# Chunk attention and a token mixer on one core: units of 512 tokens and four heads in place of 256 tokens and eight, q and k in 1 KB pieces, and transposes of 64x64

## The chip, the cores and the metric

The kernel runs on one core of a Trainium2 chip. The metric is the device time in microseconds of that core, the median of the runs. The engines are named as the profile names them: PE (matmul; PEld is its weight load), DVE and ACT (vector and scalar work; both can read PSUM), POOL (here it issues the loads, which cast float32 to float16 on the way) and SP (here it issues the stores). PSUM has 8 banks of 512 float32 per partition, called `ps` in the code.

## The reference, cut to what matters

```python
# q, k, v: (8 batches, 8 heads, 576 tokens, 64); each chunk of 64 tokens attends to itself
scores = scale * np.matmul(q_c, k_c.transpose(0, 1, 2, 4, 3))     # 9 chunks of 64x64 a head
scores = scores - np.max(scores, axis=-1, keepdims=True)
attn = np.exp(scores)
attn = attn / (np.sum(attn, axis=-1, keepdims=True) + 1e-09)
out = np.matmul(attn, v_c)
...
x = out.transpose(0, 2, 1, 3).reshape(B, S, H * D)                # (8, 576, 512)
wq = x @ w_q                                                      # (8, 576, 64)
wk = x @ w_k
W_tok = scale * np.einsum('bsd,btd->bst', wq, wk)
mixed = np.einsum('bst,btd->bsd', W_tok, x)
return (np.maximum(mixed, 0.0) @ w_out).astype(np.float32)
```

## The kernel before, in words

The mixer is linear up to its relu, so for each batch the kernel first makes the 64x512 matrix G = wk^T x over all 576 tokens, and then relu(wq G) w_out for each stretch of tokens.

**Units.** A unit is a pair of 128-token tiles of one batch, with all eight heads: two for each batch (512 tokens), and four "rest" units, each with the last 64 tokens of two batches. That makes 20 units (`pairs`, line 148). A unit is worked in these steps; each step is one entry of a graph and is emitted as a whole:

- `tq` (line 365, `tqr` at 349 for a rest): q, and likewise k, lies with two tokens in one partition (`R = 2`). PE transposes 128x64 pieces by the identity, 16 for each of q and k; two go side by side into the two halves of PSUM's partitions.
- `qb`, `kt` (line 287, the helper `copy`): q goes to SBUF in two copies of 64 partitions, into a block-diagonal tile `qbd` that is zero elsewhere; k in one copy.
- `S` (389): 16 matmuls of 64 columns with the block-diagonal q as 128x128 weights, so that two heads come out of one matmul. Scores fill two banks.
- `mx`, `sub` (402, 412), both DVE: row maximum over the keys, then the subtraction, which also puts the tokens of a chunk back into order (it reads PSUM in order and writes with a step of 2). `exp` (422), ACT.
- `E` (434): 8 transposes of 128x128. `et` (287): copy to SBUF.
- `V` (464), two steps: 16 matmuls of 64x64 weights and 65 columns each, in the four quarters of the array by turns; the 65th column of v is 1 and gives the denominator. `den`, `rec`, `x` (477, 481, 491), all DVE: add 1e-9, reciprocal, multiply into `xs`.
- `xT`, `xt` (511, 287), `pj`, `wt` (521, 287), `wkT`, `wk` (538, 287): x transposed, projected by w_q and w_k at once, and wk turned back.

When all units of a batch are there, `G` (575) and its two copies `gx`; then for each unit `mix` (616), `rm` (629 on DVE, 631 on ACT; relu with the scale), `out` (643, four matmuls of 512 columns for 128 tokens), `osb` (287, the eviction) and the store (226). An `out` step with i = 1, or of a rest unit, is stored as two halves of 64 rows, since its two chunks lie apart or in other order: 40 stores have 64 rows, 16 have 128.

**What sets the order.** `ORDER` (line 20) is written out by hand: each word is a step's number, the engine (P, V or S; `copy` steps may go to either V, DVE, or S, ACT) and the PSUM bank. Words `w7` or `n7` are idle matmuls of 512 or 128 columns that keep PE's clock up. Each engine works through its own instructions in this order and waits on semaphores. `LOADS` (line 60) is the order of the loads; POOL issues them in this order through `graph.queue` (97), each as soon as the words before it have emitted the step that frees its buffer. There are 7 homes for q and k pairs and 10 for v pairs. The first q and k come through SP as float32 and are cast (line 303). `GATE` (66, 280): a small DMA on SP reads the last load's data; all stores stand behind it on SP's queue, so no store starts before the loads are done. Up to 24 output tiles (`osb`) can wait.

Of the kernel before, what the change touches and what calls it, by code (L numbers as in the profile page):

```python
# [9 lines left out]
F16 = mybir.dt.float16  # L10
# [10 lines left out]
5V 4V 0S 1S w7 w7 w7 w7 n7 n7 n7 n7 n7 n7 n7 n7 n7 n7 n7 n7 6P0 2V 3S 7V w7 n7 n7 n7 n7 n7 n7 n7 n7  # L21
9P1 8S n7 n7 34P2 10S 35S 11P0 31P2 12V 32S 13V 33S w7 w7 n7 n7 n7 n7 n7 n7 n7 n7 56P3 36P4 58S 14S
59V 37V n7 n7 n7 91P2 57S 15P0 92S 60P3 38V 94P1 93S 95S 61V 39S w7 n7 n7 n7 n7 n7 96P4 62V 116P1
16S 97V 40P3 63S 21P6 41S 64P0 98V 118S 17P2 65S 18V 22V 99S 66P4 23V 19V 24V 117S 67V 20V 100P0
42P6 68V 46P2 69V 25P1 43V 47V 70P4 44V 26S 45V 101S 48V 71S 49V w5 n5 n5 n5 n5 n5 119P1 102P4 120S
106P2 50P0 107V 108V 27P1 109V 51S 72P6 28S 103V 52P0 73S 74P1 29P6 121P2 53S 75V 54P0 30V 163P1
122V 55S 76P0 164S 160P6 77V 104V 78S 105V 79P0 123V 80S 110P7 85P4 124S 83P0 86V 111S 125P1 84S
81P4 126V 161S 162S 127P0 131P2 112P5 128V 132V 129V 133V 89P6 130V 113S 82S 134V 165P0 90S 114P4
135P2 166V 87P3 136S 137P2 167V 88S 138S 210P5 139P2 295P3 115V 140S 211V 168S 141P0 212V 185P1 213V
142S 298V 214P2 143S 169P4 186S 215V 144P6 170V 188P0 145S 216V 150P4 189S 187V 175P6 146P2 296S  # L30
176V 217S 297V 177V 190P0 178V 147S 380P3 151S 191V 218P2 245P6 219V 247S 299P4 192V 248P5 246S
148P2 249S 300V 193S 152P0 301V 149S 382V 220P6 171P4 153S 194P1 221V 172V 173V 383S 154P2 222V 195S
223V 381S 174V 200P0 155S 196P6 224P3 201V 156P4 202V 197V 225S 203V 179P2 226P3 198V 180S 199V
250P0 302S 181P2 157V 204P6 251V 182S 303P4 205S 158P2 304S 227S 252V 183P5 384P4 184S 206P3 159S
228P5 330P6 207S 229V 208P0 332V 273P1 209S 253S 230P0 385V 358P2 331S 231V 270P3 274V 232S 271S
386V 233P0 359S 272V 305P6 333P4 234S 306V 307V 275P2 308V 334S 239P0 276V 237P5 240S 254P4 277V
238S 335P0 255S 241P5 336V 278S 355P2 242S 256P6 337V 279P3 357S 309P4 280S 243P5 257V 258V 356S
259V 281P0 310S 285P2 244S 260P6 282V 235P4 283V 286V 338S 261V 284V 311P5 262V 287V 360P0 263V 312S
236S 339P5 288V 387S 264P6 361V 289P2 265S 388P3 313P4 290S 266P6 362V 291P2 267S 340S 268P6 415P7
389S 314V 269S 292S 390P0 345P4 293P2 391V 418P3 346V 294S 347V 363S 392V 348V 315P2 443P6 393V 316S  # L40
341P4 419S 394P0 342V 364P1 317S 343V 395V 416S 318P2 344V 396P0 365S 417V 324P4 349P1 325V 350S
444S 397V 366P4 319S 370P0 440P6 367V 368V 371V 509P7 372V 441S 373V 420P2 369V 442S 320P0 421V 511S
351P1 510S 374P4 352V 321S 445P6 422V 375S 326P1 446V 376P0 423S 322P2 327S 377V 424P3 447V 398P0
353P1 378P4 399S 484P5 354S 487P0 379V 323S 425V 400P1 448S 488V 430P2 426P6 485S 328P4 431V 432V
427V 433V 486S 449P0 428V 329V 402S 489P2 401S 429V 403P4 490V 434P1 404S 409P6 450S 491V 556P4 410S
512P5 553P0 557V 435S 455P2 451P6 513S 405P1 456V 457V 492S 452V 458V 514P4 453V 406S 454V 407P2
555S 515V 459P1 554S 493P3 460S 408V 436P0 494S 461P1 516V 437S 495P2 462S 499P6 578P0 496V 500V
517S 497V 581P1 501V 498V 558P4 502V 580S 463P2 518P3 559V 579S 438P6 503P7 582S 411P0 504V 464S
439S 519S 465P1 560V 412S 520P2 466S 524P6 413P0 521V 467S 525V 522V 523V 561S 474P4 526V 583P2 527V
475S 505P1 584V 562P6 506S 468P4 528P1 585V 469S 476P7 414S 480P4 529V 470P2 586S 481V 507P0 530P1  # L50
477V 563S 587P3 508S 531S 564P4 588V 568P0 532P6 482P7 533S 569V 565V 471S 570V 566V 571V 534P3 483S
567V 589P0 536S 593P6 572P2 590V 535S 591V 594V 592V 478P4 573S 595V 596V 549P0 574P2 550V 597P3
575S 543P6 598V 472P0 544S 479V 599P1 547P2 600V 601P1 576P3 537P4 602S 577S 545P6 538S 603P1 548S
551P3 605V 473V 541P2 552S 604V 546S 606P0 542S 612P4 607V 539P3 613S 618P6 608P0 619S 540S 620P1
609V 616P2 621S 610P0 617V 614P1 611S 615S
# [5 lines left out]
k1 q1 rk0b rq0b rk0a rq0a q3 k3 q4 v0a v0b rv0b v1a rv0a v1b k4 v3a v3b wq wk k5 q5 wo v4b v4a rk1b  # L61
rq1b rq1a rk1a q6 k6 v5b v5a q8 k8 rv1a rv1b v6a v6b q11 k9 q9 k12 k11 v8a v14a q16 v9a q12 v9b v8b
v19a k15 k14 v12a q14 v11a v11b v12b v19b q15 v18a q17 q18 v14b k18 k17 v15b v17b k16 v17a q19 v15a
v18b v16a k19 v16b
"""
GATE = 76
# [28 lines left out]

# [18 lines left out]
def kernel(  # L114
# [10 lines left out]
    nc = tc.nc  # L125
# [3 lines left out]
    C, P, R, G = 64, 128, 2, 32  # L129
    NF = DM // P  # L130
    HP = H // 2
    NPB = S // (2 * P)
# [4 lines left out]
    NB2 = B // 2  # L137
# [10 lines left out]
    pairs = []  # L148
    for b in range(B):
        pairs += [(b, m) for m in range(NPB)]  # L150
        if b in (0, 2, 3, 4):
            pairs.append((b, None))
    index = {bm: u for u, bm in enumerate(pairs)}
    rests = [u for u, (b, m) in enumerate(pairs) if m is None]
    whole = [u for u, (b, m) in enumerate(pairs) if m is not None]
    both = [(0, 1)] + [(b, b + 3) for b in (2, 3, 4)]
    rest_of = {b: (rests[n], c) for n, bs in enumerate(both) for c, b in enumerate(bs)}
    NQK, NV = 7, 10

    RINGS = {  # L160
        "qb": 3, "kt4": 3, "kt2": 2, "mx2": 3, "mx1": 2, "sh2": 2, "sh1": 1, "es2": 2, "es1": 1,
        "et2": 2, "et1": 1, "xs2": 8, "xs1": 4, "xt2": 2, "xt1": 1, "wt2": 8, "wt1": 4, "wk": 8,
        "wkr": 4, "rm2": 4, "rm1": 1, "g16": 5, "den": 4, "rec": 4, "osb": 24,
# [10 lines left out]
    qbd = [const.tile([P, HP, 4, 2, C], F16, name=f"qbd{n}") for n in range(RINGS["qb"])]  # L174
    g16 = [const.tile([P, DM], F16, name=f"g16{n}") for n in range(RINGS["g16"])]
    wkr = [const.tile([P, 2, DH], F16, name=f"wkr{n}") for n in range(RINGS["wkr"])]
    qk_homes = [const.tile([P, 2, H, R * D], F16, name=f"qk{n}") for n in range(NQK)]
    wo = const.tile([P, NF, DM], F16, name="wo")
    v_all = const.tile([P, 2 * NV, H, VW], F16, name="v_all")
    v_rest = const.tile([P, NB2, H, VW], F16, name="v_rest")  # L180
    gate = const.tile([1, 1], F16, name="gate")
    qkr = const.tile([P, 2, NB2, H, D], F16, name="qkr")
    ones = const.tile([P, 512], F16, name="ones")
    for t, value in [(ones, 1.0)] + [(t, 0.0) for t in qbd[:2]]:
        nc.vector.memset(t[:], value)
# [8 lines left out]


    qk = {u: qk_homes[n % NQK] for n, u in enumerate(whole)}
    st, wide, turned, valued = {}, {}, {}, {}

    def rows_of(x, u):
        b, m = pairs[u]  # L200
        return x[b, :, 2 * P * m : 2 * P * m + 2 * P, :].rearrange("h (p r) d -> p h (r d)", r=R)

    def load_qk(u, t):
        nc.gpsimd.dma_start(qk[u][:, t], rows_of((q, k)[t], u))  # L204

    def v_home(u, i):
        return v_all[:, 2 * (whole.index(u) % NV) + i]

    def load_v(u, i):
        b, m = pairs[u]  # L210
        of = v[b, :, 2 * P * m + P * i : 2 * P * m + P * i + P, :].rearrange("h p d -> p h d")
        nc.gpsimd.dma_start(v_home(u, i)[:, :, 0:D], of)  # L212

    def load_rest(x, part, c):
        b, n = (c, 1) if part == 0 else (2 + 3 * c, NB2 - 1)
        of = (q, k, v)[x][b : b + n, :, S - C : S, :].rearrange("b h p d -> p (b h) d")
        to = v_rest if x == 2 else qkr[:, x]
        to = to[half(c), part : part + n, :, 0:D].rearrange("p n h d -> p (n h) d")
        nc.gpsimd.dma_start(to, of)

    held = []

    def store(to, of):

        if "open" in st:
            nc.sync.dma_start(to, of)
        else:
            held.append((to, of))

    def open_gate(of):  # L230
        nc.sync.dma_start(gate[:], of)
        st["open"] = True
        for to, x in held:
            nc.sync.dma_start(to, x)

    def load_w(i, x):
        nc.gpsimd.dma_start(wqk[:, :, i, :], x.rearrange("(f p) j -> p f j", p=P))

    for t, x in enumerate((q, k)):
        for i in range(2):  # L240
            wide[t, i] = ring([P, DM], F32, "osb")
            rows = rows_of(x, 0)[:, 4 * i : 4 * i + 4]
            nc.sync.dma_start(wide[t, i][:].rearrange("p (h e) -> p h e", e=R * D), rows)
            graph.loads.append((f"f{t}{i}", "SP", 512))
# [5 lines left out]
    for t in wkr:  # L250
        nc.gpsimd.memset(t[:], 0.0)
# [456 lines left out]
```

## Time and profile before

| | |
|---|---|
| runs | 138.96, 141.2, 141.28 us; median 141.2 |
| span of the profiled execution | 138.2 us; its own time is not listed apart from the span |
| busy | PE 121.3, DVE 107.2, ACT 99.9, POOL 70.3 us |
| DMA | 25.11 MB in 86185 packets, 182 GB/s over the span |
| POOL's queue (loads) | 78544 packets, 14.29 MB as they land |
| SP's queue (first loads, stores) | 7618 packets, 10.49 MB |

How to read it: a row of a group is line, engine, operation, output<-input, shapes, count | busy us, mean ns of one | idle time ahead of it and what ended it. The mean of a PE row contains its way through the array; what one matmul costs in a row of them is read from the chain of work that ended last, whose rows are start, duration and count. A stage row is from:to, length, then busy us and count of PE, PEld, DVE, ACT and POOL, the granted clock, the DMA share and GB/s. Loads count with the bytes that land, half of what is read, because they are cast to float16.

### The profile page before, as it was taken

The numbers are of one execution on the slowest core, as the hardware profiler recorded it, in microseconds if no ns is written. First come the engines' busy times: TensorE is split into PE (matmuls) and PEld (weight loads), VectorE is DVE, ScalarE is ACT, GpSimd is POOL, SyncE is SP. The second block draws the span as 40 slices with busy tenths as digits, with TensorE's granted clock in tenths as the row PEclk, the third lists the DMA queues.
The fourth block names the chain that finished last, engine by engine and source line by source line (L and its number), as shares of the span: only waits on it lengthen the run. The fifth ranks groups of instructions, "written<-read, shape, count | busy, mean of one in ns | idle before, by whom it ended". The sixth has DMA issues, their size and how long they took to land.

```text
span 138.2 us, 5123 instructions
## 1 busy us (share of the span) xinstructions
PE 121.3 (88%) x2184; PEld 88.0 (64%) x2184; DVE 107.2 (78%) x212; ACT 99.9 (72%) x186; POOL 70.3 (51%) x93
## 2 busy tenths in 40 slices
PE   5839996998999999999999949998999999999800
PEld 2627784785578757777677838677785866645300
DVE  6443699879698999999998969999999989644200
ACT  3333699656868988889998939697999886468400
POOL 8999999965658479587959867200000000000000
PEclk9975799999999999999999999999999999999995
DMA  3999999999999999999999999992788596888895
GB/s 113 228 162 178 164 158 162 187 180 137 143 165 175 150 163 183 174 166 168 173 165 167 177 173 170 165 142 22 197 249 254 155 312 196 283 267 181 235 283 143
DMA packets 86185, 25.11 MB, mean 182 GB/s; under 512 B 78994, under 2 KB 81554, under 8 KB 86162
## 3 DMA queue, kind: packets, MB, share of 16 engines
q0 software_dynamic: 78544, 14.29, 140.4%
q1 hardware_dynamic: 7618, 10.49, 26.3%
q8 instruction: 17, 0.28, 0.8%
q14 instruction: 6, 0.05, 0.1%
HBM read 29.62 MB, written 9.44 MB: 283 GB/s over the span
## 4 chain that ended last, share of the span: by engine, by line
PE 67%; ACT 15%; DVE 5%; DMA 5%; issue 3%; SPq 1%; ACTq 0%
PE ps L643 20%; PE ps L365 9%; PE ps L521 6%; PE ps L389 5%; PE ps L616 5%; PE ps L511 5%; PE ps L434 5%; DMA osb<-in_k_dram 5%; PE ps L464 5%; ACT es L422 4%; PE ps L575 3%; ACT qbd L287 3%; ACT et L287 2%; DVE sh L412 2%; PE ps L675 2%
## 5 line engine op out<-in xcount | busy, mean ns | idle before, releaser
L643 PE MATMUL ps<-wo,rm 128*128 128x512 f16 x144 | 36.2, 379 | 0.3 <-ACT rm L631 0.2
L212 POOL DMA_DIRECT2D v_all<-in_v_dram x32 | 28.4, 894 | 7.9 <-DMA v_all<-in_v_dram 2.0
L402 DVE TENSOR_REDUCE mx<-ps 128x16 f32<-128x1024 f32 (+1 forms) x20 | 22.2, 1111 | 4.6 <-PE ps L389 4.1
L491 DVE TENSOR_TENSOR xs<-ps,rec 128x512 f16<-128x512 f32 x36 | 24.1, 686 | 0.5
L365 PE MATMUL ps<-ident,qk 128*64 128x128 f16 x512 | 21.3, 230 | 3.2 <-DVE qk L287 1.6
L365 PEld LDWEIGHTS <-qk 128*64 128x64 f16 x512 | 16.8, 115 | 6.3 <-ACT qk L287 1.8
L422 ACT ACTIVATE es<-sh 128x1024 f16<-128x1024 f32 (+1 forms) x20 | 19.5, 977 | 1.4 <-DVE sh L412 1.1
L643 PEld LDWEIGHTS <-rm 128*128 128x128 f16 x144 | 12.5, 98 | 11.6 <-ACT rm L631 0.8
L412 DVE TENSOR_TENSOR sh<-ps,mx 128x1024 f32<-128x1024 f32 x16 | 19.6, 1222 | 0.3
L287 ACT COPY osb<-ps 128x512 f32<-128x512 f32 x29 | 16.7, 587 | 3.5 <-PE ps L643 3.3
L287 ACT COPY qbd<-ps 64x512 f32<-64x512 f32 (+1 forms) x31 | 16.9, 551 | 3.3 <-PE ps L365 1.9
L631 ACT ACTIVATE rm<-ps 128x1024 f16<-128x1024 f32 (+1 forms) x14 | 13.9, 996 | 3.4 <-PE ps L616 3.2
L204 POOL DMA_DIRECT2D qk<-in_k_dram x15 | 13.5, 902 | 4.4 <-DMA wo<-in_moe_w_out_dram 1.8
L204 POOL DMA_DIRECT2D qk<-in_q_dram x15 | 13.4, 896 | 2.8 <-DMA qk<-in_q_dram 0.9
L287 ACT COPY xt<-ps 128x512 f32<-128x512 f32 (+1 forms) x16 | 8.7, 547 | 5.4 <-PE ps L511 5.1
L616 PE MATMUL ps<-wt,g 128*128 128x256 f16 (+1 forms) x96 | 11.2, 246 | 1.6 <-issue 1.0
L389 PE MATMUL ps<-kt,qbd 128*128 128x64 f16 x288 | 12.1, 196 | 0.1
L389 PEld LDWEIGHTS <-qbd 128*128 128x128 f16 x288 | 10.6, 100 | 1.7 <-issue 0.5
L464 PEld LDWEIGHTS <-et 64*64 64x64 f16 x576 | 7.5, 107 | 6.1 <-issue 2.3
L511 PE MATMUL ps<-ident,xs 128*128 128x128 f16 x144 | 11.1, 219 | 0.0
L521 PE MATMUL ps<-xt,wqk 128*128 128x256 f16 (+1 forms) x80 | 10.8, 261 | 0.0
L434 PE MATMUL ps<-order,es 128*128 128x128 f16 x128 | 9.8, 219 | 1.0 <-ACT es L422 1.0
(59 smaller groups left out, 176.6 us busy)
## 6 DMA issues: line engine op xcount, KB each, us to landing
out_dram<-osb SPq DMA_DIRECT2D x40, 128.0 KB, 2.6
v_all<-in_v_dram POOLq DMA_DIRECT2D x32, 128.0 KB, 8.5
out_dram<-osb SPq DMA_DIRECT2D x16, 256.0 KB, 2.6
qk<-in_k_dram POOLq DMA_DIRECT2D x15, 256.0 KB, 8.9
qk<-in_q_dram POOLq DMA_DIRECT2D x15, 256.0 KB, 8.9
osb<-in_q_dram SPq DMA_DIRECT2D x2, 256.0 KB, 3.1
osb<-in_k_dram SPq DMA_DIRECT2D x2, 256.0 KB, 5.9
wo<-in_moe_w_out_dram POOLq DMA_DIRECT2D x1, 512.0 KB, 8.7
```

The lines of the kernel that those rows point to most:

```text
L204: nc.gpsimd.dma_start(qk[u][:, t], rows_of((q, k)[t], u))
L212: nc.gpsimd.dma_start(v_home(u, i)[:, :, 0:D], of)
L287: (nc.vector.tensor_copy if eng == DVE else nc.scalar.copy)(to, of)
L365: nc.tensor.transpose(tp[half(o), j, :, r, :], of, ident[:])
L389: nc.tensor.matmul(sp[:, i, j, c, :], lhsT=st["qb", u][:, j, x].rearrange("p o s -> p (o s)"), rhs=st["kt", u][:, j, x * C : x * C + C], s ...
L402: nc.vector.tensor_reduce(mx[:], scores(), axis=AX.X, op=ALU.max)
L412: nc.vector.tensor_tensor(out=sh[:].rearrange("p x (g r) -> p x r g", r=R), in0=in_banks(bs, 512).rearrange("p i (x r g) -> p (i x) r g", ...
L422: nc.scalar.activation(es[:].rearrange("p x s -> p (x s)"), st["sh", u][:].rearrange("p x s -> p (x s)"), AF.Exp, scale=scale_attn,)
L491: nc.vector.tensor_tensor(out=to, in0=xp()[:, :, :, 0:D], in1=by, op=ALU.mult)
L521: nc.tensor.matmul(pj, lhsT=wqk[:, f].rearrange("p i j -> p (i j)"), rhs=st["xt", u][:, f, :], start=(f == 0), stop=(f == NF - 1),)
L616: nc.tensor.matmul(ma[:, o, f, s], lhsT=st["g", bb][:, (2 * o + f) * P : (2 * o + f) * P + P], rhs=st["wt", u][:, s], start=True, stop=True,)
L643: nc.tensor.matmul(in_banks(bo, DM)[:, 0], lhsT=rm[:, f, i * P : i * P + P], rhs=wo[:, f, :], start=(f == 0), stop=(f == NF - 1),)
```

## The change

It rewrites the units, and with them nearly every function; `Step`, `Banks`, `Graph` and the launch stay.

- **Units.** A unit is 512 tokens of one batch and four heads (`HQ`), two for each batch; a rest unit is the last 64 tokens of four batches, all heads (batches 8 and 9 in the code). That makes 18 units of 32 chunk-heads each. The order of the batches is 0, rest 8, 1, 2, 3, rest 9, 4 to 7 (`TOKENS`).
- **q and k** lie with four tokens in one partition (`R = 4`): a piece is 1 KB of DRAM, and one load brings q or k of a whole batch. Batch 0 comes half through SP (as float32), half through POOL. There are 4 homes. v has a place for every batch (no reuse).
- **Transposes** (`QUART_T` names all units): 64 of 64x64 a unit, in the quarters of the array, q and k together into two banks; **one copy** of 128x1024 takes them to SBUF (`qkT`). There is no block-diagonal tile. `S` is 32 matmuls of 64x64 weights and 64 columns in quarters.
- **The subtraction** reads PSUM with the four tokens' order undone: `p (r g)` as `p g r`, so neighbours in its output are 16 words apart in PSUM, in runs of four; it writes without a step.
- `pj`, `wt`, `wkT`, `wk`, `mix` and `rm` are worked for a batch (512 columns) rather than for a unit.
- **Loads held in line** (`look`, `INLINE`): before a load is issued, POOL copies one element of the load ahead of which, by the table `rates`, 7 us of loading lie; so POOL waits there until that load has landed.
- **Stores.** All whole units' outputs are stored as 128 rows; only the four rest outputs go in halves. After the last load, stores go by turns to POOL's and SP's queue. The gate stands at load 60 of 63 (the second piece of v of batch 7).
- **A new order**: 505 steps in place of 622, 60 idle matmuls of 512 columns, 26 of them before the first transpose and none after the first words of batch 2.

```diff
-GATE = 76
+GATE = 60
+YS = ((0,), (1,))
+OUTS = (1, 1, 1, 1)
+MIX = 2
+QUART_T = [(b, w) for b in range(10) for w in range(2)]
+INLINE = 7.0
...
-    C, P, R, G = 64, 128, 2, 32
+    C, P, R = 64, 128, 4
+    HQ = H // 2
+    G = C // R
+    NT = 4
...
+    TOKENS = [0, 8, 1, 2, 3, 9, 4, 5, 6, 7]
+    NQK = 4
...
+    def load_qk(t, b, part):
+        nc.gpsimd.dma_start(qk[b][:, t, hs(part)], rows_of((q, k)[t], b)[:, hs(part)])
...
+    def send(to, of):
+        if st.get("last") and count["pool"] < count["sp"]:
+            count["pool"] += 1
+            nc.gpsimd.dma_start(to, of)
+        else:
+            count["sp"] += 1
+            nc.sync.dma_start(to, of)
...
+    def look(of):
+        nc.gpsimd.tensor_copy(peek[0:1, :], of)
...
+        rates = {256: 14.5, 512: 22.9, 1024: 39.7, 2048: 73.0}
+        line.append((n * rates[size] / 16000, last))
+        seen = next((m for m in range(n_load, -1, -1) if sum(x for x, _ in line[m:]) > INLINE), -1)
+        if 0 <= seen < n_load and INLINE:
+            graph.queue.append((lambda of=line[seen][1]: look(of()), lambda: []))
...
-                for j in range(HP):
-                    for r in range(R):
-                        for o in range(2):
-                            of = qk[u][:, t, 2 * j + o, r * D : r * D + D]
-                            nc.tensor.transpose(tp[half(o), j, :, r, :], of, ident[:])
...
+            def pe_t(eng):
+                tp = in_banks(bt, 512, F16).rearrange("p a (t j y r g) -> p a t j y r g", t=2, j=2, y=4, r=R)
+                for t in (1, 0):
+                    for j in range(2):
+                        for n in range(4):
+                            for a, o in QUARTERS:
+                                if rest < 0:
+                                    of = qk[b][half(a), t, HQ * w + 2 * j + o, n * D : n * D + D]
+                                    to = tp[half(o), a, t, j, :, n, :]
...
+                                nc.tensor.transpose(to, of, ident[half(a), half(a)])
...
+        def ev_t(eng):
+            tt = ring([P, 2, 2, 2, 4, C], F16, "qkT")
+            to = tt[:].rearrange("p b j a y s -> p b (j a y s)").bitcast(F32)
+            copy(eng, to, in_banks(bt, 512))
...
+            for j in range(2):
+                for y in range(4):
+                    for o, a in QUARTERS:
+                        nc.tensor.matmul(
+                            sp[half(a), o, j, y, :],
+                            lhsT=turned_at(0, o, a, j, y),
+                            rhs=turned_at(1, o, a, j, y),
...
-                    out=sh[:].rearrange("p x (g r) -> p x r g", r=R),
-                    in0=in_banks(bs, 512).rearrange("p i (x r g) -> p (i x) r g", r=R, g=G),
...
+                to, of = to.rearrange("p x (g r) -> p x g r", r=R), of.rearrange("p x (r g) -> p x g r", r=R)
+                by = st["mx", u][:, :, None, None].broadcast_to([P, 16, G, R])
+            nc.vector.tensor_tensor(out=to, in0=of, in1=by, op=ALU.subtract)
```

More of the change, by code (lines that the diff above doesn't have):

```diff
@@ L190, in in_banks @@
         return a.bitcast(F16) if dtype == F16 else a
-    def half(i):
-        return slice(C * i, C * i + C)
[L196 to L207, printed above, removed]
@@ new lines @@
+            last = lambda i="qk".index(key[1]): wqk[0:1, NF - 1, i, 0:1]
+        graph.loads.append((key, "POOL", n, size))
+        rates = {256: 14.5, 512: 22.9, 1024: 39.7, 2048: 73.0}
[3 more added lines that the diff above has]
+            graph.queue.append((lambda of=line[seen][1]: look(of()), lambda: []))
+        graph.queue.append((emit, lambda after=after: [s for bw in after for s in turned[bw]]))
@@ new lines, in attention @@
+        turned[u] = [n]
+        n = add("qkT", u, EITHER, ev_t, [n], reads=bt, makes=[tags["qkT"]])
+        n = add("S", u, PE, pe_s, [n], QUART, [bs], size=32, uses=[tags["qkT"]])
+        n = add("mx", u, DVE, ev_mx, [n], reads=bs, makes=[tags["mx"]])
+        n = add("sub", u, DVE, ev_sub, [n], reads=bs, makes=[tags["sh"]], uses=[tags["mx"]])
+        n = add("exp", u, ACT, ev_exp, [n], makes=[tags["es"]], uses=[tags["sh"]])
+        n = add("E" if whole_e else "Eq", u, PE, pe_e, [n], FULL if whole_e else QUART, [be], size=8 if whole_e else 32, uses=[tags["es"]])
@@ new lines, in ev_w @@
+            if rest >= 0:
+                for a in range(2):
+                    copy(eng, wk_rest[rest][half(a), :, a, :], of[half(a)])
+            else:
+                st["wk", b] = ring([P, NT, DH], F16, "wk")
+                copy(eng, st["wk", b][:], of)
+        z = "" if rest < 0 else "r"
+        deps = [st["xt_n", (b, w)] for w in range(2 if rest < 0 else 1)]
+        n = add("pj" + z, b, PE, pe_p, deps, FULL, [bp], size=4, uses=mine + [("load", "wq"), ("load", "wk")])
+        n = st["wt_n", b] = add("wt" + z, b, EITHER, ev_p, [n], reads=bp, makes=wtag)
@@ L668, with relu @@
-    for u, (b, m) in enumerate(pairs):
-        attention(u, *turns(u))
-        project(u)
-        if m is None or m == NPB - 1 and b not in (0, 2, 3, 4):
-            mixing(b)
+        mix_out(b)
+        both = [batch_at(r, a, x) for a in range(2)]
+        if all(("g", z) in st for z in both):
+            mix_rest(r, x, both)
+    def relu(eng, to, of):
+        if eng == DVE:
+            nc.vector.tensor_scalar(to, of, scale_moe, 0.0, op0=ALU.mult, op1=ALU.max)
+        else:
+            nc.scalar.activation(to, of, AF.Relu, scale=scale_moe)
@@ new lines, in mix_out, with pe, ev @@
+    def mix_out(b):
+        rtag = ("ring", "rm", b)
+        uses = [("ring", "wt", b), ("ring", "g16", b)]
+        rm_n = []
+        for o in range(NF // MIX):
+            bm = Banks(MIX)
+            def pe(eng, o=o, bm=bm):
+                for f in range(MIX):
+                    nc.tensor.matmul(
+                        in_banks(bm, TOK)[:, f].rearrange("p (a i s) -> p a i s", a=2, i=NT),
+                        lhsT=st["g", b][:, (MIX * o + f) * P : (MIX * o + f) * P + P],
+                        rhs=st["wt", b][:].rearrange("p i a s -> p a i s"),
+                        start=True,
+                        stop=True,
+                    )
+            def ev(eng, o=o, bm=bm):
+                if ("rm", b) not in st:
+                    st["rm", b] = ring([P, NF, TOK], F16, "rm")
+                relu(eng, st["rm", b][:, MIX * o : MIX * o + MIX], in_banks(bm, TOK))
+            n = add(f"mix{MIX}", b, PE, pe, st["g_n", b], FULL, [bm], size=MIX, uses=uses)
+            rm_n.append(add(f"rm{MIX}", b, EITHER, ev, [n], reads=bm, makes=[rtag]))
+        at = 0
+        for n in OUTS:
+            s = slice(P * at, P * at + P * n)
+            rows = out[b, s, :].rearrange("(p i) e -> p i e", i=n)
+            rm = lambda f, i, s=s, n=n: st["rm", b][:, f, s].rearrange("p (s i) -> p i s", i=n)[:, i, :]
+            outs(b, at, n, rm_n, rtag, rm, lambda osb, rows=rows: store(rows, osb[:]))
+            at += n
@@ new lines, in outs, with pe_o, ev_o @@
+    def outs(b, at, n, deps, rtag, rm, send):
+        bo = Banks(n)
+        def pe_o(eng):
+            for i in range(n):
+                for f in range(NF):
+                    nc.tensor.matmul(
+                        in_banks(bo, DM)[:, i], lhsT=rm(f, i), rhs=wo[:, f, :], start=(f == 0), stop=(f == NF - 1)
+                    )
+        def ev_o(eng):
+            tag = "osb" if n == 1 else "osb2"
+            osb = ring([P, n, DM], F32, tag)
+            copy(eng, osb[:], in_banks(bo, DM))
+            send(osb)
+        n1 = add(f"out{n}", (b, at), PE, pe_o, deps, FULL, [bo], size=4 * n, uses=[rtag, ("load", "wo")])
+        tag = ("ring", "osb" if n == 1 else "osb2", (b, at))
+        add(f"osb{n}" if b < REST else "osbr", (b, at), EITHER, ev_o, [n1], reads=bo, makes=[tag])
@@ L674, in idle @@
+    done = set()
+    for b in TOKENS:
+        for w in range(2 if b < REST else 1):
+            attention(b, w)
+        project(b)
+        done.add(b)
+        for z in WHOLE:
+            if ("g", z) not in st and z in done and REST + z // 4 in done:
+                mixing(z)
     def idle(i, cols):
```

679 lines of the change are left out of this document (313 added, 366 removed).

## The prediction

> **What bounds the kernel now.** I read the page's head, then busy time by stages, the waits of SP's queue, the end of the chain, and SP's last issue.
>
> ```profile
> span 138.2 us, 5123 instructions
> ...
> PE 121.3 (88%) x2184; PEld 88.0 (64%) x2184; DVE 107.2 (78%) x212; ACT 99.9 (72%) x186; POOL 70.3 (51%) x93
> ```
> ```profile
> 57.50:96.00 38.50, 35.96 (x760) 27.98 (x759) 35.39 (x70) 32.29 (x64) 23.54 (x27) 1.00 1.95 157
> 96.00:131.00 35.00, 34.82 (x533) 22.80 (x527) 26.79 (x54) 27.06 (x51) 0.00 (x0) 1.00 0.79 227
> ```
> ```profile
> SPq L231 <- DMA v_all<-in_v_dram: 92.7, 1, 92.7
> ```
> ```profile
> 126.51 4.33 PE ps L643 x20
> 130.86 0.58 ACT osb L287
> ```
> ```profile
> 134.68 0.54 SPq L226 DMA_DIRECT2D out_dram<-osb  x1
> ```
>
> No engine alone is the bound. From 57.5 to 96 us PE is busy 35.96 of 38.5 and DVE 35.39, while loads still arrive; from 96 to 131 PE is busy without a break (34.82 of 35). The 92.7 us that SP waits, ending at 95.5, are the gate: all loads take that long, and no store leaves earlier. After it 56 stores follow each other on SP; 40 of them have only 64 rows, and one of those costs SP about as much as one of 128. So the tail is long: PE ends at 130.84, the last eviction at 131.44, the last store is issued only at 134.68, and the span ends 3.5 us behind that issue. The three runs lie 0.8 to 3.1 us above this span. The profiled execution's own time is not given beyond its span, so I add 1.9, the middle, to every span. 2% (2.8 us) is about what a measurement here can tell from no change.
>
> **Loads.** The reference's sizes fix the pieces. Before: 32,768 of 512 B (q and k), 46,080 of 256 B, 512 of 2 KB. After: 16,384 of 1 KB in place of the first. The last column of a stage row is GB/s.
>
> ```profile
> 30.00:35.00 5.00, 4.40 (x67) 3.08 (x65) 4.92 (x8) 3.25 (x6) 2.46 (x3) 1.00 3.43 141
> 50.00:55.00 5.00, 4.90 (x106) 3.17 (x104) 4.80 (x15) 4.26 (x10) 3.97 (x5) 1.00 1.91 181
> ```
>
> By LOADS, and some 9 us from issue to landing, 30 to 35 us holds almost only 256 B pieces (128 B land as fp16) and 50 to 55 us mostly 512 B ones. So 16 engines x 128 B / 141 = 14.5 ns a piece, and 16 x 256 / 181 = 22.6. With the 2 KB pieces on the same line (some 71 ns) this makes 41.8 + 46.3 + 2.3 = 90.4 us; the gate saw the end at 95.5, so 5 us are start and last landing. No row has 1 KB pieces. No gain per byte would be 45 ns; another step by the ratio 22.6/14.5 would be 35; the straight line through the two rows gives 39, which I take, the middle (the diff's own table says 39.7). The whole stream is then 84.0 + 5 = 89 us, 6.4 less.
>
> What counts is when PE can begin batch 4, since the new order works batch by batch and its PE steps up to there (31 us of work) are fewer than the loads allow. Up to q4 there are 29,696 pieces of 256 B (26.9 us), 10,240 of 1 KB (25.0) and wo (2.3): 54.2, and with most of the 5 us of lead 58.5. Ends: 56 at 35 ns, 62.3 at 45.
>
> **PE.** An unbroken stretch of the chain gives the costs.
>
> ```profile
> 98.23 0.47 PE ps L389 x16
> 98.69 0.86 PE ps L643 x4
> 99.56 0.45 PE ps L511 x8
> 100.00 0.45 PE ps L434 x8
> 100.45 0.94 PE ps L521 x8
> 101.39 0.38 PE ps L464 x32
> 101.77 1.01 PE ps L365 x32
> ```
>
> Removed: a unit's 32 transposes of 128x64 (L365, 1.01 us) and 16 block-diagonal score matmuls (L389, 0.47). Added: 64 transposes and 32 scores as 64x64 quarters. The trace's only quartered work is L464, 32 in 0.38 us: 12 ns each with 65 columns; the new ones have 64. The other end is 29 ns, L389's price for 64 columns unquartered. I take 12: T 0.76, S 0.38 a unit. Everything else on PE keeps its columns in fewer, wider steps (512 columns 0.215, 256 half of that). Over 18 units PE has some 6 us less.
>
> From T of batch 4 on the new ORDER holds 32 out steps (27.5 us), 20 V of 16 quarters (3.8), 12 mix (5.3), 11 xT (4.95), 9 E (4.05), 8 T (6.1), 8 S (3.0), 6 G (3.3), 5 pj (4.4) and small ones (2.2): 64.6 us. The pace at which PE gets through such work is read from 57.5 to 131 us of before:
>
> ```profile
> L643 PE MATMUL ps<-wo,rm 128*128 128x512 f16 x110 | 27.5, 379 | 0.0
> L365 PE MATMUL ps<-ident,qk 128*64 128x128 f16 x288 | 10.6, 221 | 0.3 <-ACT rm L631 0.2
> L616 PE MATMUL ps<-wt,g 128*128 128x256 f16 x48 | 7.2, 273 | 1.2 <-issue 1.0 <-ACT g L287 0.2
> L511 PE MATMUL ps<-ident,xs 128*128 128x128 f16 x88 | 6.7, 219 | 0.0
> L521 PE MATMUL ps<-xt,wqk 128*128 128x256 f16 x44 | 6.4, 272 | 0.0
> L434 PE MATMUL ps<-order,es 128*128 128x128 f16 x80 | 6.1, 219 | 0.0
> L389 PE MATMUL ps<-kt,qbd 128*128 128x64 f16 x152 | 6.1, 193 | 0.0
> L464 PE MATMUL ps<-v_all,et 64*64 64x65 f16 x320 | 5.1, 195 | 1.0 <-DVE rm L629 0.9 <-ACT qbd L287 0.2
> ```
>
> At the chain's prices these counts are 23.7 + 9.1 + 5.3 + 5.0 + 4.8 + 4.5 + 4.5 + 3.8 = 60.7, with the smaller groups some 66.5 us of work in 73.4: a pace of 0.906. Its upper end is the 0.99 of the last 35 us. The new kernel has as much to do on PE from there but less on DVE and ACT, and DVE was as full as PE in the slower half; so I take the middle, 0.95. PE ends at 58.5 + 64.6/0.95 = 126.5 us (123.8 to 129.8 by the pace, and -2.5 to +3.8 by the pieces).
>
> **DVE and ACT.**
>
> ```profile
> L491 DVE TENSOR_TENSOR xs<-ps,rec 128x512 f16<-128x512 f32 x36 | 24.1, 686 | 0.5
> ...
> L412 DVE TENSOR_TENSOR sh<-ps,mx 128x1024 f32<-128x1024 f32 x16 | 19.6, 1222 | 0.3
> ...
> L287 ACT COPY qbd<-ps 64x512 f32<-64x512 f32 x27 | 15.5, 578 | 2.2 <-PE ps L365 1.9
> ...
> L631 ACT ACTIVATE rm<-ps 128x1024 f16<-128x1024 f32 x13 | 13.3, 1027 | 3.4 <-PE ps L616 3.2
> ...
> L477 DVE TENSOR_SCALAR den<-ps 128x8 f32<-128x8 f32 x36 | 5.0, 156 | 2.5 <-PE ps L464 2.1
> ...
> L410 DVE TENSOR_TENSOR sh<-ps,mx 128x512 f32<-128x512 f32 x4 | 2.7, 683 | 0.1
> ```
>
> Three copies a unit (two qbd of 64 partitions, one kt, each 512 columns) become one of 128x1024. 16 x 3 x 0.58 and some 4 for the rest units are 32 us; 18 at L631's 1.03 are 18.5. Memsets of the block-diagonal tiles go (some 3 us), wider wt and wk copies save as much. By V and S in the new ORDER and the rows of before, DVE's 174 instructions come to 96 us (102 before neighbours overlap), ACT to some 92. This saving shows only through PE's pace.
>
> The subtract stays 128x1024, but now reads PSUM with a step of 16 words, in runs of 4, where it read in order. Low end: L412's 1.22. High end: L410 and L412 give 1.05 ns an element and 144 fixed; den reads 8 elements 65 words apart in 156, so some 1.5 at most, or 1.7 us a subtract: +8 us of DVE. x skips a word after each 64 at no charge (686 against 683). I take 1.22, den and x being nearest. DVE has no slack: the last x must come 17.9/0.95 = 18.9 us before PE's end, at 107.6, and DVE's 89.5 us up to there fill the time from 11 us at 0.92 (35.39/38.5). Each 0.1 us more a subtract ends 2 us later.
>
> **Waits, stores, order.** Small POOL copies hold each load until one some 7 us of work earlier has landed. Behind them on POOL stand all later loads, for which T and V wait. At the tightest, four v loads (3.7 us) are still in flight when q or k is issued. I cost the hold at nothing while that cover lasts. Stores become 32 of 128 rows and 8 halves, half of them issued by POOL, which was idle by then (0.00 busy from 96 us). Tail: eviction 0.58, up to one store ahead 0.7, the 3.5 us from issue to end: 4.8 against 7.4. The 60 idle matmuls stand before batch 2, where PE waits for loads anyway.
>
> Sum: 126.5 + 4.8 = 131.3 span, 6.9 less than 138.2; with 1.9, 133.2, say **133 us**.
>
> **Rivals.**
>
> ```profile
> GB/s 113 228 162 178 164 158 162 187 180 137 143 165 175 150 163 183 174 166 168 173 165 167 177 173 170 165 142 22 197 249 254 155 312 196 283 267 181 235 283 143
> ```
> ```profile
> wqk<-in_moe_w_q_dram POOLq DMA_DIRECT2D x1, 64.0 KB, 5.5
> ```
>
> 1. *Everything keeps up* and the stores end it: gate at 87 us, 9.44 MB at an estimated 270 GB/s (the fuller slices at the end of the first row), 35 us, and 3.5: 125.5 span, 127.4 us. For it: all engines have less to do. Against: PE would have to end by 121.
> 2. *The hold runs the DMA queues dry.* The 64 KB wqk load, 0.46 us of moving, landed 5.5 us after issue, behind others; if 4.5 of it is latency, each hold leaves 0.8 us idle. Eight q and k loads precede T of batch 4: 6.4 us, 139.6 us. Against: in an empty queue the first packet should be sooner. Were 1 KB pieces no cheaper per byte (the change then not doing what it says), 3.8 us: 137.
> 3. *Slower: the stepped subtract costs double* (2.30 us): 19.4 us more on DVE, which then sets the last x: 11 + 108.9/0.92 = 129.4; + 18.9 + 4.8 + 1.9 = 155 us. It decides from 1.22 us on and reaches the old time at 1.6. For it: no row reads PSUM at such a step over many elements. Against: den and x.
> [...]
> 4. *Slower: a floor per matmul.* At 29 ns T costs 1.86 and S 0.93 a unit, 1.65 more: 5 units between batches 2 and 4 overrun the loads' cover by some 4 us, 8 later ones add 13.2/0.95 = 13.9: 151 us. Against: L464's 12 ns.
> [...]
>
> **How the numbers follow.** Forecast 0.64 (own range 128 to 138); rival 1 0.08; rival 2, or a subtract a little dearer, 0.15; rival 3 0.09; rival 4 0.04. Faster by over 2% (under 138.4): 0.64 + 0.08 = 0.72; within: 0.15; slower: 0.13. The range 126 to 142 takes in dry queues and a subtract of 1.65; it leaves out part of rival 1, and rivals 3 and 4.
>
> **What would show it.** Right: gate's wait ending near 87 us, first T of batch 4 near 58.5, the copy of T at 1.03, 64 transposes in 0.76, subtract at 1.22, PE ending near 126.5, last eviction to span's end under 5. Wrong: a subtract above 1.5, quarters above 20 ns, GB/s falling at holds, or PE idle on DVE after 60 us.

## The result, and the profile after

The changed kernel takes 158.8 us (median of four runs, 157.01 to 163.69) against 140.84 for the kernel before; over the executions compared the ratio is 1.122, 95% interval 1.109 to 1.135. The forecast was 133, with a range that ended at 142.

Some executions of one and the same kernel take over 1.5% longer than its others and are left out of the comparisons, so the lines below are from a second profiled execution of the changed kernel (157.47 us, span 155.7, clock 0.945 against 0.891 in the first), and two of the experiments rest on one and two executions. First the page.

```profile
span 155.7 us, 6771 instructions
PE 124.5 (80%) x3016; PEld 75.0 (48%) x3016; DVE 94.7 (61%) x176; ACT 94.0 (60%) x141; POOL 78.9 (51%) x157
...
PEclk9999999779959977999997799999999999999995
...
q8 instruction: 23, 0.38, 0.9%
```

PE has 3016 matmuls in place of 2184 and 31 us of idle time. Before PE ends the clock falls to half four times, 3.4 us each. The last row will matter: TensorE's own program came in 23 packets. The page of the kernel before has 17. That they are TensorE's is read from their number: its 6032 matmuls and weight loads are 23.6 times 256, the 4368 of before 17.1 times, and its stops, as shown further down, stand multiples of 256 apart.

```profile
q8 instruction: 17, 0.28, 0.8%
```

SyncE's wait for the gate, GpSimd's waits in the hold, and the two stretches of PE from T of batch 4 (69.56 us) to its end (150.3):

```profile
SPq L247 <- DMA v_all<-in_v_dram: 102.2, 1, 102.2
```

```profile
POOL peek L254 <- DMA qk<-in_k_dram: 15.2, 7, 4.5
POOL peek L254 <- DMA qk<-in_q_dram: 5.0, 5, 1.3
POOL peek L254 <- DMA v_all<-in_v_dram: 2.7, 5, 1.4
```

```profile
69.56:110.00 40.44, 29.68 (x801) 18.81 (x800) 25.06 (x48) 26.22 (x42) 22.50 (x44) 0.96 1.54 184
110.00:150.30 40.30, 40.29 (x745) 23.03 (x743) 28.55 (x53) 29.81 (x49) 7.13 (x13) 1.00 0.45 156
```

The gate opens at 105 us, not near 87. T of batch 4 starts at 69.6, not 58.5. PE then idles a quarter of the time up to 110 us (29.68 busy of 40.44; the last load has landed at 106.3), and only from there is it full, 40 us long. What the forecast said of single steps held: the subtract and the copy of T, from the groups of the page, took 1221 and 1012 ns (1220 and 1030 forecast).

```profile
L321 ACT COPY qkT<-ps 128x1024 f32<-128x1024 f32 x17 | 17.2, 1012 | 17.6 <-PE ps L387 16.7
...
L421 DVE TENSOR_TENSOR sh<-ps,mx 128x1024 f32<-128x1024 f32 x18 | 22.0, 1221 | 0.5
```

The idle time of PE is the surprise. The timeline of PE merges matmuls of one line; in brackets is the idle time ahead of a row and what released it, and "issue" means that nothing in the profile was waited for.

```profile
69.56 0.41 PE L387 MATMUL ps<-ident,qk 64*64 64x64 f16 x27
71.38 0.48 PE L387 MATMUL ps<-ident,qk 64*64 64x64 f16 x37 [1.40 <-issue]
...
78.87 0.32 PE L400 MATMUL ps<-qkT 64*64 64x64 f16 x15
82.79 0.34 PE L400 MATMUL ps<-qkT 64*64 64x64 f16 x17 [3.61 <-issue]
...
87.55 0.59 PE L387 MATMUL ps<-ident,qk 64*64 64x64 f16 x49
89.26 0.32 PE L387 MATMUL ps<-ident,qk 64*64 64x64 f16 x15 [1.12 <-issue]
...
99.08 0.48 PE L387 MATMUL ps<-ident,qk 64*64 64x64 f16 x36
102.96 0.41 PE L387 MATMUL ps<-ident,qk 64*64 64x64 f16 x28 [3.40 <-issue]
...
111.20 0.73 PE L387 MATMUL ps<-ident,qk 64*64 64x64 f16 x64
```

PE stops in the middle of a step: after 27 of 64 transposes, after 15 of 32 scores, though what the next matmuls read is there. (At 71 us this holds of k, which a T step takes first and which landed at 68.0; q came at 70.4.) Counting gaps of over 0.7 us within a step from one weight load to the next, where nothing in the profile was waited for, the trace has 8 of them, 15.7 us (before: 2, 2.4 us); 5 of the 8, 11.5 us, lie behind the start of T of batch 4. At 111 us, with the loads done, the same step runs through in 0.73 us. Two theories, then. **Hold**: GpSimd's waits let the load queue run dry, the data come late, and the rest follows. **Fetch**: PE runs out of instructions, because the packets that bring them stand behind load packets, and small matmuls use instructions up faster.

### The profile page after: what moved, and what is told of

Read it like the earlier page. It is cut to its first block, busy times and chain, and to the rows that moved or that the text cites. A ratio compares the mean times of both kernels' runs of the same rounds, so it can differ in the third digit from the quotient of the medians.

```text
span 161.9 us, 6771 instructions
## 1 busy us (share of the span) xinstructions
PE 132.5 (82%) x3016; PEld 78.9 (49%) x3016; DVE 95.1 (59%) x176; ACT 94.3 (58%) x141; POOL 79.0 (49%) x157
## 4 chain that ended last, share of the span: by engine, by line
DMA 42%; issue 34%; POOL 20%; POOLq 1%
DMA v_all<-in_v_dram 16%; DMA qk<-in_k_dram 11%; DMA qk<-in_q_dram 10%; POOL out_dram L235 6%; DMA wo<-in_moe_w_out_dram 4%; POOL v_all L215 3%; POOL peek L254 3%; POOL v_all L224 2%; POOL qkr L219 2%; POOL g L271 2%; POOL qk L211 1%; POOL wqk L227 1%; POOLq L783 0%; POOL wkr L267 0%; POOL order L263 0%
## 5 line engine op out<-in xcount | busy, mean ns | idle before, releaser
L235 POOL DMA_DIRECT2D out_dram<-osb x20 | 11.0, 549 | 45.2 <-ACT osb L321 42.4
L411 DVE TENSOR_REDUCE mx<-ps 128x16 f32<-128x1024 f32 x18 | 21.9, 1218 | 16.7 <-PE ps L400 16.7
L321 ACT COPY qkT<-ps 128x1024 f32<-128x1024 f32 x17 | 17.2, 1012 | 10.9 <-PE ps L387 10.6
L421 DVE TENSOR_TENSOR sh<-ps,mx 128x1024 f32<-128x1024 f32 x18 | 22.0, 1221 | 0.5
L427 ACT ACTIVATE es<-sh 128x1024 f16<-128x1024 f32 x18 | 19.1, 1059 | 4.9 <-DVE sh L421 4.2
L755 PE MATMUL ps<-ones 128*128 128x512 f16 x60 | 20.1, 461 | 1.7 <-DVE ones L185 1.5
L387 PE MATMUL ps<-ident,qk 64*64 64x64 f16 x1024 | 13.7, 205 | 7.9 <-issue 4.6
L387 PEld LDWEIGHTS <-qk 64*64 64x64 f16 x1024 | 11.5, 117 | 11.9 <-issue 8.0
L440 PEld LDWEIGHTS <-es 128*128 128x128 f16 x144 | 10.4, 109 | 6.0 <-ACT es L427 2.9
L660 ACT ACTIVATE rm<-ps 128x1024 f16<-128x1024 f32 x13 | 12.8, 1021 | 0.7 <-PE ps L671 0.7
L588 PE MATMUL ps<-xt,wqk 128*128 128x512 f16 (+1 forms) x40 | 12.5, 449 | 0.0
```

What stands on the lines that cost most here:

```text
L321: (nc.vector.tensor_copy if eng == DVE else nc.scalar.copy)(to, of)
L387: nc.tensor.transpose(to, of, ident[half(a), half(a)])
L411: nc.vector.tensor_reduce(mx[:], of, axis=AX.X, op=ALU.max)
L421: nc.vector.tensor_tensor(out=to, in0=of, in1=by, op=ALU.subtract)
L427: nc.scalar.activation(to, st["sh", u][:].rearrange("p x s -> p (x s)"), AF.Exp, scale=scale_attn)
L440: nc.tensor.transpose(ep[:, n], of, (order if rest < 0 else ident)[:])
```

## The experiments

All ratios are to the kernel before on the same chip, with the 95% interval.

**The changed kernel again** (no edit), to stand beside the next three.

> The changed kernel as it is, beside the runs of the next three. Three theories of the 17.6 us that it lost. Hold: the copies with which GpSimd reads a landed tile before it issues the next load let the load queue run dry, so the stream of loads ends at 104 us instead of 89 and the rest of the step work is pushed behind it. Fetch: the smaller and twice as many matmuls make TensorE outrun its own instruction transfers (the 16 KB instruction packets), which stand behind load packets; eight stops of 16.9 us together in the middle of steps. Clock: the idle time of either kind takes the clock to half, about 34 us long in the profile, and the loss is mostly that. Here all three say 157 to 159 us, with the last load landing near 104 and the stops in the middle of steps again.

157.43 us, ratio 1.123 (1.114 to 1.133). The third theory of this expectation, the clock, is too small to be most of the loss: four half-clock stretches of 3.4 us can cost 6.8 us at most, of some 17.

**No hold.**

```
-INLINE = 7.0
+INLINE = 0.0
```

> The hold is left out: loads are issued as soon as their destination is free, as in the kernel before. Nothing else changes. Theory hold: the last load lands at 88 to 92 us, the copies on GpSimd that waited 26 us are gone, and the time falls by most of the 17 us, to 140 to 146. Theory fetch: the instruction transfers now stand behind even more load packets, the stops in the middle of steps are as long or longer, and the time stays at 152 to 160 although the loads end earlier.

158.4 us, ratio 1.125 (1.111 to 1.139). SyncE's wait for the gate is 14 us shorter, and q of batch 4 has landed at 62.5 us instead of 70.4, by the packets in the trace.

```profile
SPq L247 <- DMA v_all<-in_v_dram: 87.9, 1, 87.9
```

```profile
91.62 0.85 PE L387 MATMUL ps<-ident,qk 64*64 64x64 f16 x49
94.50 0.43 PE L387 MATMUL ps<-ident,qk 64*64 64x64 f16 x15 [2.04 <-issue]
...
104.52 0.71 PE L387 MATMUL ps<-ident,qk 64*64 64x64 f16 x64
```

The theory of the hold falls as the cause by itself: all of the load time comes back and none of the kernel's. The stops inside steps grow to 20.0 us, and T of batch 4 starts at 75.6, 13 us behind its data. The T step that stops after 49 transposes here is the one that stopped after 49 in the profile above: the place in the program is the same, the time is another.

**128x64 transposes, with the hold** (a T step has 32 matmuls, as before the change), and **without it**.

```
-QUART_T = [(b, w) for b in range(10) for w in range(2)]
+QUART_T = ()
```

> The transposes of q and k are done as 128x64 blocks (half as many matmuls in a T step) instead of 64x64 quarters; the hold stays. Theory hold: the loads end at 104 as before and the time stays at 155 to 159. Theory fetch: TensorE has some 640 instructions fewer, the stops in the middle of steps fall from 16.9 to below 9 us, and the time falls to 146 to 150.

> Both edits together: no hold, and 128x64 transposes. If the hold is the whole cause it equals the run without the hold; if the instruction transfers are, it equals the run with the tall transposes alone; if both cost something the gains add up, to 134 to 140 us.

With the hold 150.86 us (one execution, so no interval; span 149.1, 6.6 below the changed kernel; three more took 153.89 to 156.21); without it 146.80 (span 145.6, 12 below the run without the hold), ratio 1.046 (1.037 to 1.054). From the waits of PE's weight loads, the time per line (sum, times, longest) that nothing explains, first with the 64x64 transposes and the hold, then with the 128x64 ones and the hold, then without the hold:

```profile
PEld L387 <- issue: 10.0, 13, 3.5
PEld L400 <- issue: 6.5, 8, 3.7
```

```profile
PEld L368 <- issue: 2.6, 7, 0.4
PEld L400 <- issue: 1.4, 5, 0.4
```

```profile
PEld L368 <- issue: 3.2, 9, 0.4
PEld L400 <- issue: 7.6, 8, 3.2
```

Larger transposes cost more PE time (1.08 us a T step against 0.73) and save 6.6 us with the hold, by that one execution, and 12 without it. With both the hold and fewer instructions no such stop is left, and what PE waits for within a step is q (8.8 us); without the hold 9.2 us of stops are left, 6.5 of them in the scores. So the two edits hang together: as I read it, the hold delays data and lets instructions through. With 64x64 transposes that is even; with 128x64 ones the delay weighs more. The sum of the gains that I had expected (134 to 140) was too much: as the hold goes, 9.2 us of stops come back.

**The hold in the kernel before.**

```
...
+        line.append((n * size / 16000, last))
+        seen = next((m for m in range(n_load, -1, -1) if sum(x for x, _ in line[m:]) > 7.0), -1)
+        if 0 <= seen < n_load:
+            graph.queue.append((lambda of=line[seen][1]: nc.gpsimd.tensor_copy(peek[0:1, :], of()), lambda: []))
```

> The kernel before, with the hold added: GpSimd reads one element of a landed tile before it issues the next load, so that at most about 7 us of loads are under way by the same estimate of load times. No other change. The hold delays the stream (with the hold 104 us, without it 92 in the changed kernel): the loads of this kernel, which ended at 95.5, then end at 103 to 110 and the time is 146 to 152. If a hold costs nothing as long as four loads are under way, as the prediction had it, 140 to 142.

144.87 us, ratio 1.032 (1.024 to 1.040): between the two answers. The gate comes 6 us later (92.7 before), and GpSimd's waits for q and k are 5.6 us in all against 20.2. This kernel's q and k loads are half as large; that this is why was not tried.

```profile
SPq L232 <- DMA v_all<-in_v_dram: 98.5, 1, 98.5
```

```profile
POOL peek L289 <- DMA qk<-in_k_dram: 3.6, 4, 1.9
POOL peek L289 <- DMA qk<-in_q_dram: 2.0, 3, 1.1
```

**More loads, no hold**: 24 loads of v issued a second time, which nothing needs. In the first form steps of batch 2 still stood behind the repeated loads in the program and waited for them.

> The changed kernel without the hold, and 24 loads of v issued once more behind the last one (batches 0 to 2, which no step reads by then): extra work that the outputs do not need, it stretches the load traffic from 92 to about 114 us. Theory fetch (TensorE's instruction packets stand behind load packets): T and S steps between 95 and 115 us, which took 0.52 us a T step without these loads, now stop in the middle, 4 to 10 us more in all, and the time is 161 to 167. If the stops belong to the early part of the order and not to the load traffic, none is seen after 95 us and the time stays at 157 to 160.

200.95 us, ratio 1.430 (1.417 to 1.444), and no verdict on the question: one V step waited 54.9 us for data.

```profile
PE ps L492 <- DMA v_all<-in_v_dram: 56.3, 2, 54.9
```

One thing it does show: after that wait no load was left, and the nine T steps from 119 us on took 0.51 to 0.77 us each from first to last start, with no stop in any step. The second form issues them only once the V steps of batches 0 to 2 stand ahead.

```
+    for b, m in [(b, m) for b in (0, 1, 2) for m in range(NT)] * 2:
...
+        after = lambda: [s for s in graph.steps if s.kind[0] == "V" and s.u[0] in (0, 1, 2)]
+        graph.queue.append((lambda b=b, m=m: load_v(b, m, ""), after))
```

> The changed kernel without the hold and with 24 loads of v issued once more behind the last one, as before, but now issued only after every V step of batches 0 to 2 stands ahead of them in the program, so that no step waits for them. The outputs do not need them; they stretch the load traffic from 92 to about 114 us. Theory fetch: TensorE's 16 KB instruction packets keep coming 6.2 to 6.6 us apart until then (without these loads 3.5 to 5.7 from 92 us on), T and S steps between 92 and 114 us stop in the middle, and the time is 162 to 167. If the stops belong to the early part of the order, the time stays at 157.5 to 160.

166.18 us, ratio 1.188 (1.184 to 1.192), as the theory of the fetch had it. (Of the 6.6 us by which PE ends later than without these loads, 1.6 stand already at 87 us, shortly after the first of them is issued.) The timeline of PE, with load traffic until 116 us:

```profile
87.31 0.32 PE L404 MATMUL ps<-qkT 64*64 64x64 f16 x15
90.19 0.34 PE L404 MATMUL ps<-qkT 64*64 64x64 f16 x17 [2.57 <-issue]
...
93.50 0.85 PE L391 MATMUL ps<-ident,qk 64*64 64x64 f16 x49
96.66 0.43 PE L391 MATMUL ps<-ident,qk 64*64 64x64 f16 x15 [2.31 <-issue]
...
108.40 0.48 PE L391 MATMUL ps<-ident,qk 64*64 64x64 f16 x36
110.36 0.41 PE L391 MATMUL ps<-ident,qk 64*64 64x64 f16 x28 [1.48 <-issue]
```

Loads that no step waits for stop PE again, after the same 15, 49 and 36 matmuls as in the changed kernel, at other times. Starts of the 16 KB packets in the trace, us:

```
no hold            ... 73.4 79.8 86.1 92.2 | 95.7 100.9 105.7 111.4 115.4   loads end at 92
with more loads    ... 73.8 81.5 87.8 94.1 101.4 107.9 114.4 | 118.7 123.0  loads end at 116
kernel before      ... 58.7 65.2 71.8 78.2 84.8 91.4 | 94.8 100.4           loads end at 95
```

Under load traffic the packets are mostly 6.2 to 6.6 us apart (the longest of these 7.7); from the bar on, as the loads end, 3.4 to 5.7. In the run without the hold, PE had issued 1217, 1985, 2753, 3265 and 3521 instructions at five places where it stopped, by the count of its rows in the trace: 449 + 256 k each time, with k a whole number. In the changed kernel 7 of the 8 stops counted above, 14.9 of the 15.7 us, stand at such a number too, to within one row. A packet has 16,384 bytes, 64 for each of 256.

**A hold of 3.5 us** in place of 7, with 64x64 transposes.

> The changed kernel with a hold of 3.5 us in place of 7: half as much load traffic is under way. Theory fetch, with the wait of an instruction packet growing with the loads under way: the packets can come closer than 5 us, the stops in the middle of steps fall from 15.7 to below 6 us, while the stream of loads ends at 112 us or later; the time is 155 to 165 by the two together. If the stops don't hang on what is under way, 12 us or more of them are left and the time is 160 to 170.

211.4 us, ratio 1.507 (1.496 to 1.517); my expectation missed by far, because I had not seen how steeply the hold grows. GpSimd waited 93 us, and the loads ended at 176 us.

```profile
POOL peek L254 <- DMA qk<-in_k_dram: 41.2, 8, 5.7
POOL peek L254 <- DMA qk<-in_q_dram: 29.9, 7, 5.0
POOL peek L254 <- DMA v_all<-in_v_dram: 15.6, 10, 2.7
```

A k or q load alone is 2.5 us by the diff's own table, so 3.5 us means one load at a time, with its way from issue to landing (6 to 8 us in the changed kernel's page) paid in full. The packets did come sooner, mostly within 2.8 us after PE had entered the last block of 256 that it had, against mostly 3 to 4.7 without a hold, and while the loads run no stop within a step stands at 449 + 256 k. One does behind the last load, after 5569 instructions:

```profile
180.19 0.28 PE L536 MATMUL ps<-ident,xs 128*128 128x128 f16 x2
182.58 0.51 PE L536 MATMUL ps<-ident,xs 128*128 128x128 f16 x6 [2.11 <-issue]
```

Its packet started 4.3 us late, amid the stores that the gate had held (384 GB/s from 180 to 184 us). So loads are not the only traffic that goes with late packets.

**Three smaller ones.** Only the first 22 idle matmuls (these stand before the first transpose, not the 26 of the section on the change); the five clears of g on VectorE (both without hold, 128x64); and the same clears moved in the kernel before.

```
-4V 0V 1S 2V 3S w0 w0 w0 w0 w0 w0 w0 w0 w0 w0 w0 w0 w0 w0 w0 w0 w0 w0 w0 w0 w0 w0 5P0 6S w2 w2 w2
...
+4V 0V 1S 2V 3S w0 w0 w0 w0 w0 w0 w0 w0 w0 w0 w0 w0 w0 w0 w0 w0 w0 w0 w0 w0 w0 w0 5P0 6S
...
```

```
+    for t in g16:
+        nc.vector.memset(t[C : 2 * C, :], 0.0)
...
-            graph.queue.append((lambda: [nc.gpsimd.memset(t[half(1), :], 0.0) for t in g16], lambda: []))
```

> No hold, 128x64 transposes, and of the 60 idle matmuls only the first 22, which stand ahead of the first unit; the 38 between later steps are left out. If they stand where TensorE waits for loads anyway, as the prediction had it, the time is that of the run with them, 146 to 148, with a longer half-clock stretch at most. If they push real work, 140 to 144. If they keep the clock up, 149 or more with 10 us or more at half clock.

> No hold, 128x64 transposes, and the five clears of the g tiles (2.4 us on GpSimd between its sixth and seventh load) done by VectorE at the start. If GpSimd's issuing bounds the first 18 us of loads, batch 1's k is issued at about 14.7 us instead of 17.1 and the time falls by 1.5 to 2.5 us, to 144 to 145.5. If the start is covered, 146 to 147.5.

> The kernel before, with only the five clears of the g tiles (2.4 us on GpSimd ahead of its ninth load) done by VectorE at the start. If GpSimd's issuing bounds its first loads too, 138.5 to 140; if the start is covered by the work that TensorE has by then, 140 to 141.5.

Without the later idle matmuls 148.97, ratio 1.064 (1.054 to 1.075), some 2 us more than with them. In the first 40 us PE was granted 0.85 of its clock in place of 0.96; first without, then with them:

```profile
0.00:40.00 40.00, 27.24 (x560) 18.57 (x562) 21.71 (x41) 18.25 (x24) 31.51 (x48) 0.85 1.62 166
```

```profile
0.00:40.00 40.00, 33.05 (x587) 18.68 (x587) 20.62 (x40) 17.61 (x22) 31.03 (x47) 0.96 1.63 166
```

They don't push real work; as I read it, they help by keeping the clock up where PE waits. The clears: 146.0, ratio 1.040 (1.031 to 1.050), not told apart from 1.046; and 0.997 (0.992 to 1.001) in the kernel before, no difference that this measures.

**The hold only from batch 4's k on**, with 128x64 transposes and the clears on VectorE.

```
+HOLD_FROM = 39
...
-        if 0 <= seen < n_load and INLINE:
+        if 0 <= seen < n_load and n_load >= HOLD_FROM:
```

> 128x64 transposes, the clears on VectorE, and the hold of 7 us only from the k load of batch 4 on. The loads of batches 0 to 3 come as early as without the hold, when TensorE waits for them; from batch 4 on TensorE is behind the loads by up to 17 us, so a later landing costs nothing, and the instruction packets come in time. If both halves hold, the 4.4 us of stops after 60 us go and the time is 142 to 145, with the last load landing at 95 to 100. If the hold costs through the loads there too, 147 to 150.

144.16 and 144.63 us (two more executions took 147.12 and 177.43), ratio 1.032 (1.026 to 1.038); the gate opens at 96.

```profile
63.50:100.00 36.50, 34.41 (x761) 22.86 (x759) 28.98 (x55) 29.54 (x47) 21.08 (x41) 1.00 1.55 179
100.00:136.90 36.90, 36.88 (x530) 20.73 (x527) 24.83 (x48) 26.66 (x44) 6.57 (x12) 1.00 0.53 187
```

PE is 94% busy while loads still run, one stop of 1.2 us is left after 60 us, and PE ends at 136.9. This is the best form of the change that I found, and it is still 3% slower than the kernel before. What makes up these 3% I did not take apart: 4 us of stops lie ahead of 60 us, and the scores in quarters, 576 matmuls where the kernel before has 288, are the same in every run here; a run with the old scores was not made.

## Why the prediction was wrong, point by point

- **"12 ns: T 0.76, S 0.38 a unit"** is right as a duration and fails as a cost. Undisturbed, a T step took 0.73 us to its last end, 0.35 less than the 128x64 form. But the step counts the array's time alone. It doubles the instructions of T (1152 matmuls in place of 576, each with a weight load), and what PE was short of under load traffic was instructions. That, not a floor per matmul, is the price of smaller matmuls: 6.6 us of the whole with the hold (by one execution), 12 without. This is the main failure. My list of rivals had nothing of the kind, though the sign was on the page: the row of instruction packets, and a row that I quoted (L616, "issue 1.0"), which is one of the two stops of the kernel before: it stands after 2753 instructions, 449 + 9 x 256.
- **"I cost the hold at nothing while that cover lasts"** failed, and rival 2 had the mechanism: GpSimd waited 22.9 us by the three rows above, q of batch 4 landed 7.9 us later, the last load 14 later (106.3 against 92.0). Its price of 0.8 us a hold (6.4 before T of batch 4) is near the 7.9; its time of 139.6 is not, since it had the loads alone. That the hold relieves the fetch, no step had.
- **"its PE steps up to there (31 us of work) are fewer than the loads allow"** failed too. The forecast started batch 4 as q of batch 4 lands. Without the hold it lay there for 13 us, and PE, with 15 us of stops behind it, came at 75.6. With the hold the last wait for data within a step before batch 4 ended at 52.8 us (q of batch 3, which landed 5.2 us later than without the hold), a stop of 2.3 us followed, and PE began T of batch 4 on k, before q had landed.
- **39 ns for 1 KB** and the stream: without the hold the last load landed near 92 us (89 forecast) and q of batch 4 at 61.4 to 62.5 (58.5, with 56 to 62.3 as bounds). In the run without the hold, q and k loads landed mostly 2.65 us behind the load ahead, 41 ns a piece. The price was near; the landing came out at the late end of the bounds.
- **The pace of 0.95** from T of batch 4 on: 64.6/0.95 = 68.0 us forecast, 80.7 measured. With the stops gone (the late hold) it is 73.4, of which the eight 128x64 T steps are 8 x 0.34 = 2.7 and one stop about 1. The other 1.7 I don't trace.
- **DVE, ACT and the tail**: the subtract at 1.22 us, the copy at 1.01, the last matmul to the span's end 5.4 us (4.8), and the run 1.8 above its span (1.9). Rival 3 falls: the stepped read of PSUM cost nothing on VectorE (1221 ns a subtract, 1222 before). Rival 4 falls: in the chain, where I read 12 ns, 64 quarters take 0.64 us, 10 ns each, far from 29.
- **Idle matmuls where PE waits anyway**: right; taking 38 of them out costs some 2 us, with the clock at 0.85 in place of 0.96.

In sum, of the 23.8 us by which PE ended late (150.3 for 126.5), 11.1 lie ahead of T of batch 4 and 12.7 behind it.

What points to the fetch is in the traces: PE stops at distances of 256 instructions, and the packets come one block of 256 ahead at most. With the n-th packet taken for the one that brings the block from 449 + 256 (n - 1) on, each of the 40 packets of the kernel before and of the first profiled execution of the changed kernel starts when PE is 0 to 257 instructions short of that block. Under load traffic some 6.2 us lie between packets in the rows above. By these rows, 256 instructions have to last 6.2 us. A T and an S step of quarters use up 192 in about 1.2 us; a matmul of 512 columns with its weight load is two in 0.22.

Left open: why a packet starts some 4 us late under load traffic (0 to 2 without, apart from the stores after the short hold), and whether it goes by the number of pieces or by their bytes.

## What to carry to other kernels

Count an engine's instructions as well as its time: while loads ran here without a hold, TensorE mostly got its next 256 instructions 6.2 us or more after the last, and halving the size of T's matmuls cost time there (12 us) though each was cheaper (64 in 0.73 us, 32 of the larger ones in 1.08). An idle stretch in the middle of a step, released by "issue", at the same place of the program in runs of different timing, was a fetch here and no wait for data. A limit on loads under way is worth pricing from both sides: too tight it starves the data (7 us: the last load 14 us later; 3.5: 84 later), too loose it starves the instructions (20.0 us of stops without it, 15.7 with it).

## What I had not expected of the hardware

- The kernel before was near the same limit: from 58 to 91 us its packets were 6.4 to 6.6 us apart, with only 2.4 us of stops.
- 64x64 transposes in quarters come 8 ns apart (64 in 0.52 us from first to last start), and so do V's 65-column quarters in the kernel before (32 in 0.26); the 12 ns of its chain row hold the end of the step too.
- One copy of a 1 x 1 element on GpSimd takes 177 ns (27 in 4.8 us); the cost of a hold is in its wait, up to 4.5 us each with 7 us under way.
